# Staged transposed keys copied by ScalarE, and input-gate rows brought by DMA, in the attention stage of an mLSTM and mixture-of-experts kernel

## The chip, the cores and the metric

The kernel runs on one core of a Trainium2 chip. The metric is the device time of one execution, in microseconds (us). Engines are named as in the profile: PE is TensorE, PEld its weight load, DVE VectorE, ACT ScalarE, POOL GpSimd, SP SyncE, which here only issues transfers (DMAs).

## What is computed

Three layers follow each other. The first is an mLSTM recurrence over B=4 batches, H=8 heads, S=768 steps and D=40 columns; its output, seen as 3072 tokens of 320 columns, goes through a mixture of 8 experts with a capacity of 384 tokens each, and then through a dense layer of 2048 columns.

```python
for t in range(S):
    m_new = np.maximum(f_gate[:, :, t] + m, i_gate[:, :, t])
    f_stab = np.exp(f_gate[:, :, t] + m - m_new)
    i_stab = np.exp(i_gate[:, :, t] - m_new)
    C = f_stab * C + i_stab * outer(v_t, k_t)
    n = f_stab * n + i_stab * k_t
    y[:, :, t] = sigmoid(o_t) * (C @ q_t) / np.maximum(np.abs(n . q_t), 1.0)
...
order = np.argsort(-flat)          # tokens are given to experts, best logit first, 384 each
out[mask] = np.maximum(x[mask] @ w1[e], 0.0) @ w2[e]
...
g = np.maximum(h, 0.0) + alpha * np.minimum(h, 0.0)
return g @ w_out
```

## The kernel before

Only the first stage, attention, is touched. It cuts the 768 steps into 9 chunks of 86 and works on 36 units: unit u is chunk c = u // 4 and batch b = u % 4, all 8 heads at once. Within a chunk the recurrence is a masked product; the state is carried from chunk to chunk as 40 more rows (126 = 86 + 40).

The loop over u (line 573) writes all engines' instructions in program order, and each engine runs its own in that order; nothing is reordered. For a unit, `score` (line 435) does these things:

- pE (line 441): two bf16 matmuls of cE (113 x 126, the left factor) with aE (113 x 344). Their product is the exponent of the gate weights. cE holds the input-gate rows of the chunk in its first 24 partitions, in three bf16 parts of 8 heads; aE holds the forget-gate sums in partitions 24 to 26.
- W (line 443): ScalarE's exponential of pE, 344 columns a time.
- pS (line 448): four fp32 matmuls of the transposed keys KT (stationary) with the queries Q.
- dk (line 450): VectorE multiplies the scores with W; GpSimd makes the state's columns (line 452).

`value` (line 456) runs for unit u-2: eight matmuls pY with dk stationary, the normalisation on VectorE, the gated product x on GpSimd (line 477) and the store of x to device memory in two transfers, of 80 rows and of 6 rows (`rows`, line 349). `turn` (line 546) transposes x of unit u-4 (pX), ScalarE copies it to xT (line 553), and `logit` multiplies a chunk of it with the router's weights (pL, line 566).

The input-gate rows of chunk c+1 are made in the units with b == 2 (line 581): `gates_rows` (line 302) moves rows to the right partitions with 12 small matmuls of a selection matrix into pc, and ScalarE copies pc to cE (line 309). The forget-gate rows come by three small transfers from ap (`load_a`, line 311), 5.4 KB each. The gates themselves are made by the generators g0, g1 (chunks 0 and 1 to 3) and g2 (chunks 4 to 8, one step a unit from unit 2 on).

KT has two buffers of 128 x 16 x 126. The last 40 of the 126 columns and the partitions from 80 on are constant and filled once: buffer 0 by GpSimd (lines 334 and 338), buffer 1 by ScalarE (lines 394 and 395). A load (line 359) writes 80 partitions x 16 pieces of 86 floats (344 bytes).

All loads of the stage and the stores of x are issued by SP in one queue, in program order: v and o-gates of later chunks at b == 2, q, k and kr (keys in rows) at b == 3, the forget-gate rows behind them, then stores of x. Between them stand the pieces r of the dense weights (`words`, line 908), which `float32_of` turns from 64-bit to 32-bit floats: ScalarE's sign of r (sg, line 926), two VectorE steps, ScalarE's Abs (line 932) and GpSimd's product (line 933). A piece is issued three pieces ahead of its use; one is used every second unit from unit 8 to 23, and one every unit from unit 24 on (lines 594 to 597).

Each transfer of SP's queue carries one of eight semaphores in turn (DMAHW0 to DMAHW7 in the order below) and waits until the transfer that had it before, eight places ahead in the queue, has landed.

The lines on loads in the loop are these; the functions follow.

```python
if b == 2 and c + 1 < NCH:
    self.gates_rows(c + 1, ps)
...
if b == 3 and c + 2 < NCH:
    load_qk(c + 2)
    load_k(c + 2)
if b == 3 and c and c + 2 < NCH:
    self.load_a(c + 2, nc.sync)
```

Of the kernel before, what the change touches and what calls it, by code (L numbers as in the profile page):

```python
# [24 lines left out]
L = 86  # L25
# [35 lines left out]
def host_constants():  # L61
    import ml_dtypes
    bf = ml_dtypes.bfloat16
    ce = np.zeros((KE, X), np.float32)
    ce[24:27, :] = 1.0
    ce[27:, :L] = np.eye(L)
    ae = np.zeros((KE, H, L), np.float32)
    for p in range(3):
        for h in range(H):
            ae[p * 8 + h, h, :] = 1.0  # L70
    ae[27:] = np.where(np.arange(L)[:, None] > np.arange(L)[None, :], -1e30, 0.0)[:, None, :]
    sel = np.zeros((32, B, 3, 24), np.float32)
    for b in range(B):
        for p in range(3):
            for h in range(H):
                sel[8 * b + h, b, p, 8 * p + h] = 1.0
    g = np.arange(128)
    return {
        "c_blk": (g[:, None] // 16 == g[None, :] // 16).astype(bf),
        "c_pre": ((g[:, None] // 16 == g[None, :] // 16) & (g[:, None] < g[None, :])).astype(bf),  # L80
        "c_tri": (g[:, None] < g[None, :]).astype(bf),
        "c_sel": sel.astype(bf),
        **steps(""), **steps("_a"),
        "c_ce": np.pad(ce, ((0, 128 - KE), (0, 0))).astype(bf),
        "c_ae": np.pad(ae.reshape(KE, H * L), ((0, 128 - KE), (0, 0))).astype(bf),
    }


def host_layout(inp):
# [22 lines left out]
    o["h_i"] = np.ascontiguousarray(inp["i_gate"].reshape(32, S))  # L112
    o["h_f"] = np.ascontiguousarray(inp["f_gate"].reshape(32, S))
# [46 lines left out]
class Kern:  # L160
# [80 lines left out]
    def gates_setup(self, p):  # L241
# [19 lines left out]
        self.aE = [p.tile([KE, B, H, L], BF, name=f"aE{r}") for r in range(3)]  # L261
# [49 lines left out]
    def load_a(self, c, eng):  # L311
        for i in range(3):
            eng.dma_start(self.aE[c % 3][24 + i:25 + i], self.ap[:, i, c * L:(c + 1) * L])

    def attention(self):
        nc, a, tc = self.nc, self.a, self.tc
        with ExitStack() as ctx:
# [7 lines left out]
            KT = [p.tile([128, 16, X], F32, name=f"k{r}") for r in range(R)]  # L325
# [8 lines left out]
            nc.gpsimd.memset(KT[0][64:], 0.0)  # L334
# [3 lines left out]
            nc.gpsimd.tensor_copy(KT[0][:2 * D, :, L:], idk[:, None, :].to_broadcast([2 * D, 16, D]))  # L338
# [16 lines left out]
            def load_qk(c):  # L355
                r = c % R
                for s in range(2):
                    nc.sync.dma_start(Q[r][D * s:D * s + D, s], a["h_q"][c, s])
                nc.sync.dma_start(KT[r][:2 * D, :, :L], a["h_kt"][c])

# [11 lines left out]
            def fill_a(r):  # L372
                nc.vector.tensor_copy(self.aE[r].rearrange("p b h l -> p b (h l)"),
                                      self.ae0[:, None, :].to_broadcast([KE, B, H * L]))
# [19 lines left out]
            nc.scalar.activation(KT[1][64:].rearrange("p g x -> p (g x)"), zero[64:].to_broadcast([64, 16 * X]), AF.Copy, scale=0.0)  # L394
            nc.scalar.activation(KT[1][:2 * D, :, L:], idk[:, None, :].to_broadcast([2 * D, 16, D]), AF.Copy)
# [38 lines left out]

            def score(u):
# [3 lines left out]
                for s in range(2):  # L439
                    pE = ps.tile([X, 4 * L], F32, name="pE", bufs=2)  # L440
                    nc.tensor.matmul(pE, self.cE[c % 3][:, b, :], self.aE[c % 3][:, b, 4 * s:4 * s + 4, :],
# [3 lines left out]
                for s in range(2):  # L445
                    pS = ps.tile([X, 4, L], F32, name="pS", bufs=2)
                    for j in range(2):
                        nc.tensor.matmul(pS[:, 2 * j:2 * j + 2, :], KT[r][:, 4 * b + 2 * s + j, :],  # L448
# [124 lines left out]
            for u in range(nu + 4):  # L573
                if u < nu:
                    c, b = units[u]
                    score(u)
                    if u < 3:
                        warm_up(u)
                    if u >= G2:
                        next(g2, None)  # L580
                    if b == 2 and c + 1 < NCH:
                        self.gates_rows(c + 1, ps)
# [7 lines left out]
                    if b == 3 and c and c + 2 < NCH:  # L590
# [740 lines left out]
```

## Time and profile before

| what | value |
|---|---|
| median of 3 runs | 808.88 us |
| lowest and highest | 806.67 and 813.15 us |
| the profiled execution's own time | 807.55 us |
| its span, first to last instruction | 805.8 us |
| PE, share of the span busy | 90% |
| PE weight loads | 85% |
| DVE, ACT, POOL | 70%, 54%, 53% |
| mean granted PE clock | 0.955 of full speed |
| transfers | 72.73 MB in 47531 packets, 26097 of them under 512 bytes |

The span is from the first instruction of the execution to the last; the time holds 1.75 us more around it. A share is the mean over stages with different limits: attention takes about the first 165 us, the routing of tokens the next 50, and the experts with the dense layer the rest. A matmul's record is modelled at its end, so a busy PE need not be at its peak. Clock is given as a share of 2.4 GHz; it has two levels, 1.0 and 0.5.

### The profile page before, as it was taken

The page shows a single profiled execution, that of the slowest core. Times are in us where ns is not written, and L with a number is a line of the kernel's source. Part 1 is how long each engine was busy: PE and PEld are TensorE (multiplying, and loading weights), DVE is VectorE, ACT ScalarE, POOL GpSimd, SP SyncE. Part 2 cuts the span into 40 slices and gives each one's busy share as a digit, 9 for nine tenths or more (in the row PEclk, how much of TensorE's full clock was granted, in tenths as well). Part 3 has the DMA queues.
Part 4 walks back from the last instruction along what each step waited for, and adds up shares of the span by engine and source line. Part 5 has one row for each costly group of instructions (what it writes and reads, how often), then busy time and mean ns, then how long its engine had stood idle before and what let it go on. Part 6 is the DMA issues. An engine that isn't in the chain of part 4 may idle for free.

```text
span 805.8 us, 14935 instructions
## 1 busy us (share of the span) xinstructions
PE 724.5 (90%) x4868; PEld 688.0 (85%) x4868; DVE 560.8 (70%) x2209; ACT 435.1 (54%) x948; POOL 423.9 (53%) x509
## 2 busy tenths in 40 slices
PE   4999989920399999998999999999999999999996
PEld 3999989810388899998999899999999999999996
DVE  8887776888778878867876986797698732322311
ACT  6575655767244572565267346525833664654463
POOL 4565654569372384267149516723941686534133
PEclk9999997955599999999999999999999999999998
DMA  8999988551230150033014004202400343100000
GB/s 190 223 221 226 207 203 209 167 139 55 96 100 2 38 153 31 1 104 118 1 43 154 26 1 120 84 19 70 128 25 1 115 142 104 40 1 25 1 1 25
DMA packets 47531, 72.73 MB, mean 90 GB/s; under 512 B 26097, under 2 KB 30193, under 8 KB 47453
## 3 DMA queue, kind: packets, MB, share of 16 engines
q1 hardware_dynamic: 44332, 62.90, 29.3%
q0 software_dynamic: 2688, 8.65, 3.4%
q8 instruction: 38, 0.62, 0.3%
q14 instruction: 41, 0.33, 0.1%
q10 hardware_dynamic: 432, 0.22, 0.1%
HBM read 62.19 MB, written 9.34 MB: 89 GB/s over the span
## 4 chain that ended last, share of the span: by engine, by line
PE 51%; DVE 13%; POOL 10%; issue 8%; ACT 5%; DMA 1%; SPq 0%; POOLq 0%; DVEq 0%; ACTq 0%
PE ph L1029 23%; PE acc L1029 11%; PE fo L1029 10%; POOL gl L1166 4%; DVE scr L155 4%; DVE rb L155 3%; POOL wt L1005 2%; PE pY L464 2%; PE pS L448 2%; DVE g L155 1%; ACT m L1159 1%; ACT gh L1165 1%; ACT m L1158 1%; POOL w_dt_float32r L962 1%; PE rb L723 1%
## 5 line engine op out<-in xcount | busy, mean ns | idle before, releaser
L1166 POOL TENSOR_TENSOR gl<-g,gh 128x384 fp32r<-128x384 f32 x127 | 128.3, 1016 | 226.5 <-ACT gh L1165 218.1
L1005 POOL TENSOR_TENSOR wt<-raw,wt 128x384 fp32r<-128x384 f32 (+1 forms) x128 | 118.3, 944 | 32.4 <-ACT wt L1004 31.9
L1029 PE MATMUL ph<-yh,wfh 128*128 128x384 f32 x384 | 132.9, 346 | 0.0
L1029 PE MATMUL ph<-yh,w_dt_float32r 128*128 128x384 f32 x360 | 122.4, 340 | 0.0
L1029 PE MATMUL fo<-wfh,gh 128*128 128x320 f32 x384 | 116.2, 312 | 0.0
L1165 ACT ACTIVATE gh<-g 128x384 fp32r<-128x384 f32 x127 | 66.0, 523 | 91.0 <-DVE g L155 87.3
L155 DVE SCALAR_TENSOR_TENSOR g<-ph,m 128x384 f32<-128x384 f32 x128 | 70.4, 555 | 61.7 <-ACT m L1159 52.6
L1029 PE MATMUL fo<-w_dt_float32r,gh 128*128 128x320 f32 x360 | 109.9, 314 | 0.0
L1029 PE MATMUL ph<-xh,wt 128*128 128x384 f32 x384 | 99.7, 343 | 0.6 <-ACT xh L1060 0.6
L1091 ACT ACTIVATE hh<-ph 128x384 fp32r<-128x384 f32 x64 | 31.5, 493 | 114.2 <-PE ph L1029 83.7
L1029 PE MATMUL acc<-hh,wt 128*128 128x384 f32 x320 | 88.6, 341 | 0.0
L1029 PE MATMUL ph<-yl,wfh 128*128 128x384 f32 x256 | 84.0, 338 | 0.0
L1029 PE MATMUL fo<-wfh,gl 128*128 128x320 f32 x384 | 79.9, 312 | 0.9 <-POOL gl L1166 0.9
L1159 ACT ACTIVATE m<-m,al 128x384 f32<-128x384 f32 x119 | 73.5, 617 | 3.9
L1158 ACT ACTIVATE m<-ph 128x384 f32<-128x384 f32 x119 | 57.5, 483 | 32.9 <-PE ph L1029 31.1
L1029 PEld LDWEIGHTS ph<-yh,wfh 128*128 128x128 f32 x384 | 72.4, 188 | 0.7 <-issue 0.3
L1029 PEld LDWEIGHTS fo<-wfh,gh 128*128 128x128 f32 x384 | 72.2, 188 | 0.5 <-ACT gh L1165 0.2
L1029 PEld LDWEIGHTS ph<-xh,wt 128*128 128x128 f32 x384 | 68.8, 189 | 1.1 <-ACT xh L1060 0.8
L1004 ACT ACTIVATE wt<-raw 128x384 fp32r<-128x384 f32 x128 | 62.9, 515 | 12.7 <-DMA raw<-in_h_we_dram 12.6
L1029 PEld LDWEIGHTS fo<-w_dt_float32r,gh 128*128 128x128 f32 x360 | 67.9, 189 | 1.3 <-issue 1.2
L1029 PEld LDWEIGHTS ph<-yh,w_dt_float32r 128*128 128x128 f32 x360 | 67.9, 189 | 0.7 <-issue 0.7
L464 PEld LDWEIGHTS pY<-v,dk 126*126 126x126 f32 (+1 forms) x576 | 67.4, 192 | 0.6
(240 smaller groups left out, 1634.4 us busy)
## 6 DMA issues: line engine op xcount, KB each, us to landing
raw<-in_h_we_dram SPq DMA_DIRECT2D x64, 384.0 KB
r<-in_h_wf_dram SPq DMA_DIRECT2D x32, 352.0 KB
xd<-x SPq DMA_DIRECT2D x36, 120.0 KB
q<-in_h_q_dram SPq DMA_DIRECT2D x18, 215.0 KB
k<-in_h_kt_dram SPq DMA_DIRECT2D x9, 430.0 KB
v<-in_h_v_dram SPq DMA_DIRECT2D x9, 410.0 KB
og<-in_h_o_dram SPq DMA_DIRECT2D x9, 400.0 KB
kr<-in_h_kr_dram SPq DMA_DIRECT2D x8, 400.0 KB
```

Of the source, the lines that this page charges most:

```text
L155: return f(out, *args, **kw)
L448: nc.tensor.matmul(pS[:, 2 * j:2 * j + 2, :], KT[r][:, 4 * b + 2 * s + j, :], Q[r][:, :, 4 * b + 2 * s + j, :], start=True, stop=True)
L464: nc.tensor.matmul(pY[:M, h, :], dk[:, h, :M], V[c % RV][:, 8 * b + h, :], start=True, stop=True)
L723: self.nc.tensor.matmul(pc, self.c_blk if w is None else w, self.cacc[:, col:col + n], start=True, stop=True)
L1004: nc.scalar.activation(w[:, :384], r, AF.Copy)
L1005: nc.gpsimd.tensor_tensor(w[:, 384:], r[:, :n], w[:, :n].bitcast(F32), op=OP.subtract)
L1029: self.nc.tensor.matmul(out, w, x, **kw)
L1091: nc.scalar.activation(hh, ph, AF.Relu)
L1158: nc.scalar.activation(m, ph, AF.Relu, scale=-1.0)
L1159: nc.scalar.activation(m, m, AF.Copy, scale=alpha)
L1165: nc.scalar.activation(gh, g, AF.Copy)
L1166: nc.gpsimd.tensor_tensor(gl, g, gh.bitcast(F32), op=OP.subtract)
```

## The change

The selection matrix and `gates_rows` stay for chunk 0 alone. For the chunks from 1 on, `load_a` issues, behind each of its three transfers to aE, one that brings 8 partitions of input-gate rows from cp to cE (8 x 4 x 86 bf16). For that the gates are laid out by head and then batch, and aE with it (113 x 8 x 4 x 86), so that pE reads four runs of 86 columns in place of one of 344. There is one buffer KT; the keys of chunk 0 are loaded to it as before, those of the later chunks go to two staging buffers KS of 80 x 16 x 86 in rows of 5504 bytes, and ScalarE copies the 4 x 86 columns of unit u+1 to KT behind unit u's exponentials (`move_k`). ScalarE's two fills of the second KT buffer are gone.

`load_a` of chunk c+2 stands behind the loads of b == 3 up to unit 13, and from unit 14 on at b == 0, one unit later in the program. Neither condition holds for chunk 3, so chunk 5's six transfers are not issued: units 20 to 23 read the gate rows that chunk 2 left there, and that part of the computation is changed.

```diff
-                sel[8 * b + h, b, p, 8 * p + h] = 1.0
+                sel[B * h + b, b, p, 8 * p + h] = 1.0
...
-        self.aE = [p.tile([KE, B, H, L], BF, name=f"aE{r}") for r in range(3)]
+        self.aE = [p.tile([KE, H, B, L], BF, name=f"aE{r}") for r in range(3)]
...
     def load_a(self, c, eng):
         for i in range(3):
-            eng.dma_start(self.aE[c % 3][24 + i:25 + i], self.ap[:, i, c * L:(c + 1) * L])
+            eng.dma_start(self.aE[c % 3][24 + i:25 + i].rearrange("o h b l -> o (h b) l"), self.ap[:, i, c * L:(c + 1) * L])
+            if c:
+                eng.dma_start(self.cE[c % 3][8 * i:8 * i + 8, :, :L], self.cp[:, i, c * L:(c + 1) * L])
...
-            KT = [p.tile([128, 16, X], F32, name=f"k{r}") for r in range(R)]
+            KT = p.tile([128, 16, X], F32, name="k")
+            KS = [p.tile([2 * D, 16, L], F32, name=f"ks{r}") for r in range(R)]
...
-                nc.sync.dma_start(KT[r][:2 * D, :, :L], a["h_kt"][c])
+                nc.sync.dma_start(KS[r] if c else KT[:2 * D, :, :L], a["h_kt"][c])
...
-                nc.vector.tensor_copy(self.aE[r].rearrange("p b h l -> p b (h l)"),
-                                      self.ae0[:, None, :].to_broadcast([KE, B, H * L]))
+                nc.vector.tensor_copy(self.aE[r], self.ae0.rearrange("p (h l) -> p h l", h=H)[:, :, None, :].to_broadcast([KE, H, B, L]))
...
-            nc.scalar.activation(KT[1][64:].rearrange("p g x -> p (g x)"), zero[64:].to_broadcast([64, 16 * X]), AF.Copy, scale=0.0)
-            nc.scalar.activation(KT[1][:2 * D, :, L:], idk[:, None, :].to_broadcast([2 * D, 16, D]), AF.Copy)
...
+            def move_k(u):
+                c, b = units[u]
+                nc.scalar.activation(KT[:2 * D, 4 * b:4 * b + 4, :L], KS[c % R][:, 4 * b:4 * b + 4, :], AF.Copy)
+
...
-                    nc.tensor.matmul(pE, self.cE[c % 3][:, b, :], self.aE[c % 3][:, b, 4 * s:4 * s + 4, :],
+                    nc.tensor.matmul(pE, self.cE[c % 3][:, b, :], self.aE[c % 3][:, 4 * s:4 * s + 4, b, :],
...
+                    if 4 <= u + 1 < nu:
+                        move_k(u + 1)
...
-                    if b == 2 and c + 1 < NCH:
-                        self.gates_rows(c + 1, ps)
+                    if b == 0 and c and c + 2 < NCH and u >= G2 + 12:
+                        self.load_a(c + 2, nc.sync)
...
-                    if b == 3 and c and c + 2 < NCH:
+                    if b == 3 and c and u < G2 + 12:
                         self.load_a(c + 2, nc.sync)
```

SP's queue at the turn from chunk 5 to chunk 6, before: the loads for chunk 7 (k, kr in 80 and 6 rows, aE), the store of unit 21's x, and the piece r that ScalarE uses in unit 27.

```order
L359 DMA k_105<-in_h_kt_dram 80x16x86 [waits DMAHW3_49]
L351 DMA kr_107<-in_h_kr_dram 80x1280 [waits DMAHW4_49,Pool_49]
L353 DMA kr_107<-in_h_kr_dram 6x1280 [waits DMAHW5_49]
L313 DMA aE_100<-ap 1x32x86 [waits DMAHW6_49]
L313 DMA aE_100<-ap 1x32x86 [waits DMAHW7_49]
L313 DMA aE_100<-ap 1x32x86 [waits DMAHW0_49]
L351 DMA xd<-x_112 80x384 [waits DMAHW1_49,Pool_49]
L353 DMA xd<-x_112 6x384 [waits DMAHW2_49]
L911 DMA r_1573<-in_h_wf_dram 128x704 [waits DMAHW3_49,DVE_49,Activation_49]
```

The same place of SP's queue now, from the keys of chunk 7 to the same piece r (aE and cE are those of chunk 8):

```order
L362 DMA ks_106<-in_h_kt_dram 80x1376 [waits DMAHW5_49,Activation_49]
L354 DMA kr_108<-in_h_kr_dram 80x1280 [waits DMAHW6_49,Pool_49]
L356 DMA kr_108<-in_h_kr_dram 6x1280 [waits DMAHW7_49]
L354 DMA xd<-x_113 80x384 [waits DMAHW0_49,Pool_49]
L356 DMA xd<-x_113 6x384 [waits DMAHW1_49]
L313 DMA aE_101<-ap 1x32x86 [waits DMAHW2_49]
L315 DMA cE_98<-cp 8x4x86 [waits DMAHW3_49]
L313 DMA aE_101<-ap 1x32x86 [waits DMAHW4_49]
L315 DMA cE_98<-cp 8x4x86 [waits DMAHW5_49]
L313 DMA aE_101<-ap 1x32x86 [waits DMAHW6_49]
L315 DMA cE_98<-cp 8x4x86 [waits DMAHW7_49]
L917 DMA r_1531<-in_h_wf_dram 128x704 [waits DMAHW0_49,DVE_49,Activation_49]
```

Before, r shares DMAHW3 with k and waits for it; now it shares DMAHW0 with the store ahead of the small transfers, and the small transfer just ahead of r shares DMAHW7 with the six rows of kr.

ScalarE's queue at unit 14 (chunk 3, b == 2), before:

```order
L443 ACTIVATE W<-pE 126x344 [waits DVE_49,PE_49,Pool_49]
L443 ACTIVATE W<-pE 126x344 [waits PE_49]
L309 ACTIVATE cE_97<-pc 24x4x86 [waits PE_49]
L932 ACTIVATE w_dt_float_852<-w_dt_float_852 128x352 [waits DVE_49]
L926 ACTIVATE sg<-r_601 128x352 [waits DMAHW3_49,Pool_49]
```

And now at unit 12, where a copy of keys stands behind the exponentials of each unit:

```order
L447 ACTIVATE W<-pE 126x344 [waits PE_49] x2
L437 ACTIVATE k<-ks_106 80x4x86
L938 ACTIVATE w_dt_float_589<-w_dt_float_589 128x352 [waits DVE_49]
L932 ACTIVATE sg<-r_377 128x352 [waits Pool_49]
L432 ACTIVATE og<-og 86x320
L433 ACTIVATE og<-og 86x320 [waits Activation_49]
L557 ACTIVATE xT<-pX 128x3x86 [waits PE_49]
```

The copy of pc with its wait for PE is gone from the units with b == 2, and a copy from KS stands in every unit; in the last unit of a chunk it also waits for the transfer to KS.

## Rows read from the trace of the kernel before

**Rows 1.** Windows of 20 us: busy us of each engine (instructions), granted clock, DMA share, GB/s.

```profile
60.00:80.00 20.00, 19.71 (x187) 18.55 (x186) 14.86 (x43) 12.06 (x32) 10.72 (x17) 1.00 0.97 229
100.00:120.00 20.00, 18.80 (x183) 17.60 (x182) 15.96 (x46) 10.62 (x28) 12.49 (x19) 1.00 0.87 204
```

**Rows 2.** PE in order of time: start, us, instruction, shapes, count [idle before].

```profile
49.14 0.63 PE L307 MATMUL pc<-cp,sel 32*24 32x86 bf16 x12
49.70 1.95 PE L464 MATMUL pY<-v,dk 126*126 126x41 f32 x16
...
86.07 0.46 PE L441 MATMUL pE<-aE,cE 113*126 113x344 bf16 x2
...
93.99 0.46 PE L441 MATMUL pE<-aE,cE 113*126 113x344 bf16 x2
...
101.54 0.46 PE L441 MATMUL pE<-aE,cE 113*126 113x344 bf16 x2
```

**Rows 3.** Waits of 106 to 122 us: who waited for whom, total us, times, longest.

```profile
ACT sg L926 <- DMA r<-in_h_wf_dram: 3.3, 1, 3.3
```

**Rows 4.** PE in order of time, units 28 and 29 and the start of 30.

```profile
118.64 0.46 PE L441 MATMUL pE<-aE,cE 113*126 113x344 bf16 x2
...
121.95 1.51 PE L448 MATMUL pS<-q,k 128*126 128x172 f32 x4 [2.27 <-ACT KL L522]
...
133.46 0.46 PE L441 MATMUL pE<-aE,cE 113*126 113x344 bf16 x2
```

**Rows 5.** Windows of 1 us, columns as in rows 1.

```profile
131.00:132.00 1.00, 1.00 (x7) 1.00 (x6) 0.66 (x2) 0.14 (x1) 0.37 (x1) 0.50 1.14 158
...
216.00:217.00 1.00, 1.00 (x6) 1.00 (x4) 0.83 (x8) 0.00 (x0) 0.00 (x0) 0.50 0.96 353
...
220.00:221.00 1.00, 1.00 (x5) 1.00 (x4) 0.91 (x3) 0.94 (x3) 0.97 (x2) 0.61 0.95 379
```

**Rows 6.** SP's queue in order of time: when a transfer was issued.

```profile
51.63 0.36 SPq L911 DMA_DIRECT2D r<-in_h_wf_dram  x1
...
67.46 0.36 SPq L911 DMA_DIRECT2D r<-in_h_wf_dram  x1
...
83.19 0.36 SPq L911 DMA_DIRECT2D r<-in_h_wf_dram  x1
...
99.10 0.36 SPq L911 DMA_DIRECT2D r<-in_h_wf_dram  x1
...
110.55 1.78 SPq L313 DMA_DIRECT2D aE<-ap  x3
...
114.02 0.27 SPq L353 DMA_DIRECT2D xd<-x  x1
116.63 0.36 SPq L911 DMA_DIRECT2D r<-in_h_wf_dram  x1
117.32 0.31 SPq L351 DMA_DIRECT2D xd<-x  x1
```

**Rows 7.** Waits of SP's queue, 106 to 121 us.

```profile
SPq L911 <- DMA k<-in_h_kt_dram: 2.3, 1, 2.3
```

**Rows 8.** ACT in order of time.

```profile
13.83 0.42 ACT L295 ACTIVATE ap<-cum 32x258 bf16<-32x258 f32 x1 [0.50 <-DVE cum L290]
...
119.90 0.53 ACT L926 ACTIVATE sg<-r 128x352 f32<-128x352 f32 x1 [3.29 <-DMA r<-in_h_wf_dram]
```

**Rows 9.** Groups by line, 12 to 165 us: count | busy us, mean ns | idle before.

```profile
L448 PE MATMUL pS<-q,k 128*126 128x172 f32 x288 | 52.8, 324 | 4.1 <-ACT KL L522 2.3 <-DVE LT L569 1.6
...
L441 PE MATMUL pE<-aE,cE 113*126 113x344 bf16 x72 | 17.9, 324 | 4.6 <-ACT k L394 2.5 <-ACT W L443 1.8 <-DMA aE<-ap 0.4
...
L932 ACT ACTIVATE w_dt_float<-w_dt_float 128x352 f32<-128x352 f32 x20 | 9.9, 495 | 0.2 <-DVE w_dt_float L155 0.2
```

**Rows 10.** Groups by line, 0 to 13 us.

```profile
L373 DVE COPY aE<-ae 113x2752 bf16<-113x2752 bf16 x2 | 1.7, 858 | 0.0
L377 DVE COPY cE<-ce 113x504 bf16<-113x504 bf16 x3 | 0.7, 273 | 0.0
```

More of the change, by code (lines that the diff above doesn't have):

```diff
@@ L111, in host_layout @@
     o["h_o"] = rows(inp["o_gate"]).reshape(NCH, L, B, DM)
-    o["h_i"] = np.ascontiguousarray(inp["i_gate"].reshape(32, S))
-    o["h_f"] = np.ascontiguousarray(inp["f_gate"].reshape(32, S))
+    for n, x in (("h_i", "i_gate"), ("h_f", "f_gate")):
+        o[n] = np.ascontiguousarray(inp[x].reshape(B, H, S).transpose(1, 0, 2)).reshape(32, S)
     wg = np.zeros((128, 3, 32), np.float32)
@@ L333, in attention @@
             self.gates_fill()
-            nc.gpsimd.memset(KT[0][64:], 0.0)
+            nc.gpsimd.memset(KT[64:], 0.0)
             ident = self.identf
@@ L337, in attention @@
             nc.vector.tensor_tensor(idk, ident[:2 * D, :D], ident[:2 * D, D:2 * D], op=OP.add)
-            nc.gpsimd.tensor_copy(KT[0][:2 * D, :, L:], idk[:, None, :].to_broadcast([2 * D, 16, D]))
+            nc.gpsimd.tensor_copy(KT[:2 * D, :, L:], idk[:, None, :].to_broadcast([2 * D, 16, D]))
             nc.gpsimd.memset(V[0][64:], 0.0)
@@ L447, in score @@
                     for j in range(2):
-                        nc.tensor.matmul(pS[:, 2 * j:2 * j + 2, :], KT[r][:, 4 * b + 2 * s + j, :],
+                        nc.tensor.matmul(pS[:, 2 * j:2 * j + 2, :], KT[:, 4 * b + 2 * s + j, :],
                                          Q[r][:, :, 4 * b + 2 * s + j, :], start=True, stop=True)
```

## The prediction

> **What bounds the kernel now.** The change touches only the attention stage, which ends at about 165 of the 805.8 us span; what follows is the same code and starts when the stage ends, so I look for the shift of that end. I read the stage by windows first, then TensorE in order of time, then the waits, then the queue of transfers.
>
> The windows show TensorE busy for 19 us and more of each 20, and the DMA engines at 0.87 to 0.97 [rows 1]. So two things are near full. In order of time, TensorE runs unit behind unit without a gap: a chunk of four takes 15.47 us, from 86.07 to 101.54 [rows 2]. The input-gate matmuls (pc, 12 of them) hold the next group up by 0.56 us, from 49.14 to 49.70 [rows 2].
>
> There is one place where TensorE is stopped. ScalarE waits 3.3 us for a piece r of the dense weights [rows 3], TensorE then stands idle for 2.27 us in the middle of unit 28 [rows 4], and its granted clock is at the lower level (1.2 GHz) until about 132 [rows 5]. The pair of units 28 and 29 takes 14.82 us from 118.64 to 133.46 [rows 4]; the pair 20 and 21, with the same groups, takes 7.92 from 86.07 to 93.99 [rows 2]. The place costs 6.9 us: 2.27 idle and some 4.6 at the lower clock.
>
> Why is r late? It is issued at 116.63 [rows 6]. The queue's waits give the keys' landing as what held it (2.3 us) [rows 7]: the order of the queue shows every transfer waiting for the one eight places ahead, and for this r that is k. The r of one loop to the r of the next is 15.9 us (83.19 to 99.10) and then 17.5 (99.10 to 116.63) [rows 6], against 15.47 for TensorE. **So SyncE's queue with its transfers is a loop of its own, a little slower than TensorE's**, which falls behind until r is too late, when from unit 24 on a piece is wanted every unit and not every second.
>
> **The change, part by part**, against the profiled execution's own time of 807.55 us (the median of the runs shown is 1.3 above it).
>
> *Input-gate matmuls.* Eight groups go: 8 x 0.56 = 4.5 us of TensorE's own time. Seven lie ahead of unit 28 (3.9 us), one behind it. With them go eight ScalarE copies of pc, which no one waits for.
>
> *The keys' transfer.* 80 partitions by 16 pieces of 344 bytes become 80 rows of 5504. Of before, the second q had landed at 114.02 (the six-row store waits for it), k at 116.63 and the 80 rows of kr at 117.32 [rows 6]: k takes 2.6 us after q, kr's rows of 5120 bytes 0.7 after k. The new load costs between 0.7 and 2.6 us. I take 1.5, since kr's 0.7 overlaps the end of k: 1.1 us are saved.
>
> *Six small transfers for three.* Before, three of them took 1.78 us of the queue, 0.6 each, while k was on its way [rows 6]: hidden. Now six stand ahead of r, and the sixth waits, eight places back, for the six-row piece of kr, which lands after k. So r comes at 117.32 (kr) - 1.1 (shorter keys) + 0.3 (six-row piece, about one issue of 0.31) + 0.6 (the sixth's issue) = 117.1: each loop is 0.5 us longer, not shorter. Ends: with the sixth's wait already over, r follows the keys and the loop is 1.1 shorter; with the keys' load no faster and all three added issues in series (1.8), 117.32 + 0.3 + 1.8 = 119.4, 2.8 longer. The trace is nearest to 0.5, because the new transfers have the size and kind of the old three. The Trainium skill (DMA: Bandwidth & Descriptors, Rules for kernel authors) asks to coalesce small transfers, as under 64 KB one pays mostly overhead; charged in series at the fixed 2 us of that page three more would cost 6 us a loop, and 24 us over four loops. No row here bears that out: the three old ones lie beside k.
>
> *Four loops* end in an r between 51.63 and the r at 116.63 (those at 67.46, 83.19 and 99.10, and this one [rows 6]): 4 x 0.5 = 2.0 us later, less 1.1 once for the key loads that come ahead of the first of them: **r is issued 0.9 us later, at 117.5.** From issue to ScalarE's start took 3.27 us (116.63 to 119.90 [rows 6, 8]); TensorE resumes at 121.95 + 0.9 = 122.85. It arrives there 3.9 us earlier than before, so its idle grows from 2.27 to some 7.1 us. What the seven groups gave goes into that wait.
>
> *The lower clock.* I take the same 4.6 us. Ends: after a long idle stretch, with TensorE busy from 216 on, the upper clock returned in the slice 220 to 221 [rows 5]; some 4.8 us at half speed would cost 2.4, so 2.2 less; a second fall elsewhere, 4.6 more.
>
> *The copies on ScalarE.* 32 copies of 80 by 344. The nearest row is the 128x352 one of line 932, 495 ns [rows 9], so some 0.48 each by the count of elements: 32 x 0.48 = 15.4 us, over 32 units of 3.7 us. ScalarE is busy 10.6 to 12.1 us in 20 [rows 1], four fifths of them at most with the copies; in a chunk 1.9 us come and 0.45 (the pc copy) goes. Cost 0. Without that cover, all 15.4. Each copy is issued one unit ahead; at a chunk's start it waits for the keys' landing, and output gates, xT and the next exponentials queue behind it. The keys of chunk 6 had landed at 99.10 (its r waits for them), 2.4 us ahead of unit 24's first matmul at 101.54 [rows 2, 6]. With 6 x 0.56 = 3.4 us of that gone and 0.5 for the copy, up to 1.5 us of wait moves there; TensorE has 7 us to lose before unit 28, so it costs 0.
>
> *Start.* The two ScalarE fills of the second key buffer go, but the operation behind them waits for VectorE at 13.83 [rows 8]: 0. VectorE's fill of the left factor now reads runs of 86 elements: before, 2752 elements took 858 ns, 504 took 273 [rows 10], both in four runs; 0.26 ns an element leaves 0.14 us. If that is paid by run, 32 runs cost 1.0 us more a fill, two of them on the way to the first scores; if not, nothing. I take 0.15 each, since an instruction has a fixed part as well: +0.3, ends 0 and +2. The scores' first matmul (pE) reads four runs of 86 columns; pS reads two such runs and has the same mean, 324 ns, as pE [rows 9]: 0.
>
> **Sum:** +0.9 (r) - 0.56 (the group behind unit 28) + 0.3 (start) = +0.6, or 808.2 us by the profiled execution. Since the median stood 1.3 above it, I predict 808.5. About 1%, 8 us, is what a measurement of this kernel can tell from no change.
>
> **The rivals.**
>
> *The loop keeps TensorE's pace.* If keys and kr land about as much sooner as TensorE runs ahead (1 us a loop: the 1.1 saving without the sixth's wait), the stall keeps its size and the gain stays: 807.55 - 4.5 = 803. For it: the shorter keys. Against it: the order of the queue. Chance 0.2.
>
> *The stall goes too.* 807.55 - 4.5 - 6.9 = 796. For this r must be issued 3.3 + 3.9 = 7.2 us earlier, 1.8 in each of four loops, more than the keys' part can give unless the 0.7 us of kr is its true cost (1.9). Chance 0.12.
>
> *Slower: the small transfers lengthen the loop.* With 2.8 us a loop, r comes 4 x 2.8 = 11 us later: 807.55 + 11 - 0.6 = 818. It decides from the point where a loop is over 2.3 us longer, as the end then moves by more than 8. The place is the six issues ahead of r, each held by a landing; that the long rows bring nothing (the change does not do what it says) belongs here. For it: DMA engines at 0.9 and a queue that waits on landings everywhere [rows 1, 7]. Against it: there is no such stall by the three old ones. Chance 0.13; the skill's rule above would end here, and has no chance of its own beyond that.
>
> *The forecast*, within 804 and 812: 0.55.
>
> **How the numbers follow.** Faster by over 1%: the second rival and a little of the first, 0.13. Slower by over 1%: the upper three quarters of the third, 0.1. Within: 0.77. The range leaves out the second rival and the upper part of the third: 800.5 to 815, which also holds the ends of clock and start one at a time.
>
> **What would show it.** In the profile after: no pc after the first group, chunks of about 14.9 us on TensorE up to unit 23; r's of the queue still 16 us or more apart, with waits for kr or for the small transfers ahead of them; ScalarE's wait for r near unit 27 of 7 us or more and one stretch of lower clock behind it. I am wrong if that wait is 3.3 us or less, if the r's come under 15.5 us apart, or if TensorE waits at the chunks' starts for the copies.

## The result: 12 us slower, and the profile after

The changed kernel takes 822.8 us (median; 821.1 at best) against 811.0 for the kernel before on the same chip: ratio 1.015, 95% interval 1.010 to 1.020. I had predicted 808.5, 800.5 to 815, most likely no change: wrong. The profiled execution took 830.5 us (span 827.9). The first matmul of the routing code, which follows the attention stage, starts at 191.25 instead of 170.93 us, so nearly all of the 22 us that the spans differ by lie in the stage.

TensorE in order of time, in the profile after (start, us, instruction, shapes, count, idle before it):

```profile
42.11 0.47 PE L445 MATMUL pE<-aE,cE 113*126 113x344 bf16 x2
42.41 0.75 PE L452 MATMUL pS<-q,k 128*126 128x172 f32 x4
44.60 0.85 PE L452 MATMUL pS<-q,k 128*126 128x172 f32 x4 [1.45 <-DVE LT L573]
...
54.81 0.78 PE L445 MATMUL pE<-aE,cE 113*126 113x344 bf16 x2
...
61.41 0.78 PE L445 MATMUL pE<-aE,cE 113*126 113x344 bf16 x2
...
113.04 0.47 PE L445 MATMUL pE<-aE,cE 113*126 113x344 bf16 x2
...
127.76 0.47 PE L445 MATMUL pE<-aE,cE 113*126 113x344 bf16 x2
```

In the kernel before, TensorE's stop at the same place and the window behind it (columns as in [rows 1]; the last three figures are granted clock, DMA share and GB/s):

```profile
44.96 0.85 PE L448 MATMUL pS<-q,k 128*126 128x172 f32 x4 [0.51 <-DVE LT L569]
```

```profile
44.00:60.00 16.00, 15.49 (x156) 14.73 (x154) 12.56 (x36) 11.60 (x30) 10.42 (x16) 1.00 0.88 210
```

Windows of 1 us in the profile after:

```profile
46.00:47.00 1.00, 1.00 (x8) 1.00 (x7) 0.51 (x2) 0.00 (x0) 0.38 (x1) 0.58 1.00 292
47.00:48.00 1.00, 1.00 (x7) 1.00 (x7) 0.03 (x1) 0.00 (x0) 0.00 (x0) 0.50 1.05 235
...
100.00:101.00 1.00, 1.00 (x8) 1.00 (x7) 0.89 (x2) 0.00 (x0) 0.00 (x0) 0.61 0.01 2
```

Three things are to be seen. First, the gain is there: with the pc groups gone, a chunk at the upper clock takes 127.76 - 113.04 = 14.72 us, where [rows 2] gave 15.47. Second, TensorE stops for 1.45 us in unit 9, where VectorE's copy LT frees a buffer of PSUM (the memory that TensorE writes to), and from 46 to 101 us its clock is at the lower level (1.2 GHz), though it is busy all the time; a unit then takes 61.41 - 54.81 = 6.60 us instead of 3.4. In the kernel before the same stop was 0.51 us and the clock stayed up. Third, the queue. Its list in order of time, and ScalarE's wait for r, which answers to [rows 3, 6]:

```profile
132.08 0.54 SPq L313 DMA_DIRECT2D aE<-ap  x1
132.93 0.74 SPq L315 DMA_DIRECT2D cE<-cp  x1
134.89 0.53 SPq L313 DMA_DIRECT2D aE<-ap  x1
136.48 0.73 SPq L315 DMA_DIRECT2D cE<-cp  x1
137.93 0.52 SPq L313 DMA_DIRECT2D aE<-ap  x1
138.50 0.73 SPq L315 DMA_DIRECT2D cE<-cp  x1
139.34 0.36 SPq L917 DMA_DIRECT2D r<-in_h_wf_dram  x1
```

```profile
ACT sg L932 <- DMA r<-in_h_wf_dram: 4.4, 1, 4.4
```

From the first of the six to r it is 139.34 - 132.08 = 7.3 us; before, from the first of the three to r, with two stores between them, it was 116.63 - 110.55 = 6.1 [rows 6]. r comes 18.8 us after the r of the loop before (120.52), and ScalarE's wait for it near unit 28 is 4.4 us instead of 3.3. TensorE waits there for ScalarE's copy KL, which stands behind the sign of r in ScalarE's order. So there were two suspects, and my theory at first was the clock: that the longer stop in unit 9 lowers it (Theory 1). Its rivals were the queue, held up by the six (Theory 2, later A), and ScalarE's key copies (Theory 3, later C). The profile alone can't tell them apart, because at half the clock TensorE also gives the queue time.

### The profile page after: what moved, and what is told of

Same layout as the page of the kernel before. It is cut to its first block, busy times and chain, and to the rows that moved or that the text cites. A ratio compares the mean times of both kernels' runs of the same rounds, so it can differ in the third digit from the quotient of the medians.

```text
span 827.9 us, 14821 instructions
## 1 busy us (share of the span) xinstructions
PE 743.4 (90%) x4772; PEld 708.5 (86%) x4772; DVE 563.7 (68%) x2209; ACT 441.3 (53%) x970; POOL 422.8 (51%) x509
## 4 chain that ended last, share of the span: by engine, by line
PE 48%; DVE 13%; POOL 9%; issue 7%; ACT 4%; DMA 3%; SPq 0%; POOLq 0%; DVEq 0%; ACTq 0%
PE ph L1035 22%; PE acc L1035 10%; PE fo L1035 10%; POOL gl L1172 4%; DVE scr L155 4%; DVE rb L155 3%; POOL wt L1011 2%; PE pY L468 2%; DVE g L155 1%; ACT m L1165 1%; PE pS L452 1%; ACT gh L1171 1%; DMA q<-in_h_q_dram 1%; ACT m L1164 1%; POOL w_dt_float32r L968 1%
## 5 line engine op out<-in xcount | busy, mean ns | idle before, releaser
L468 PEld LDWEIGHTS pY<-v,dk 126*126 126x126 f32 (+1 forms) x576 | 80.7, 222 | 0.1
L468 PE MATMUL pY<-v,dk 126*126 126x41 f32 (+1 forms) x576 | 79.0, 305 | 0.0
L481 POOL TENSOR_TENSOR x<-xn,og 86x320 f32<-86x320 f32 x35 | 30.2, 862 | 79.8 <-ACT W L447 33.3
```

The lines of the kernel that those rows point to most:

```text
L468: nc.tensor.matmul(pY[:M, h, :], dk[:, h, :M], V[c % RV][:, 8 * b + h, :], start=True, stop=True)
L481: eng.tensor_tensor(xt[:, :DM].rearrange("p (h d) -> p h d", h=H), xn, OG[c][:, b].rearrange("p (h d) -> p h d", h=H), op=OP.mult)
```

## The experiments

All times are medians, and ratios are to the kernel before on the same chip, with 95% intervals. "r to r" is the mean over the four loops that end in the r of unit 28, from the queue's list (before: 16.25 us, from [rows 6]).

| kernel | us | ratio | r to r, us |
|---|---|---|---|
| change | 822.8 | 1.015 [1.010, 1.020] | |
| change again (e14_after) | 821.7 | 1.011 [1.007, 1.015] | 19.0 |
| e1_keys: keys alone | 808.8 | 0.997 [0.994, 1.001] | 15.6 |
| e2b_gates: gate rows alone | 822.7 | 1.018 [1.011, 1.024] | 19.6 |
| e3_lt_act: change, LT on ScalarE | 817.4 | 1.008 [1.005, 1.011] | 18.2 |
| e4_before_stop: before, longer stop | 810.0 | 0.999 [0.995, 1.003] | |
| e5_dummy: e1 + 3 unused transfers | 821.2 | 1.017 [1.010, 1.024] | 17.8 |
| e11_tiny: the same, one piece each | 820.0 | 1.014 [1.008, 1.020] | 17.9 |
| e12_tiny_pool: the same, by GpSimd | 810.4 | 1.001 [0.997, 1.005] | 16.3 |
| e9_rows_pool: change, six by GpSimd | 808.0 | 0.996 [0.992, 0.999] | 14.6 |
| e8_dram: change, two for six | 813.7 | 1.003 [1.000, 1.006] | |
| e10_best | 805.4 | 0.995 [0.992, 0.997] | 15.2 |

### One part at a time

e1_keys has the staged keys and their copies alone, and pc and the three aE transfers as before.

> Only the keys' part of the change: staged rows of 5504 bytes and the 32 ScalarE copies; gate rows by matmuls (pc) and the queue's order as in the kernel before. Theory 1, the clock: the loss of 12 us comes from TensorE's stop of 1.45 us in unit 9 (0.51 before), behind which the granted clock stays at 0.5 for 54 us; that stop grew because the pc groups are gone and TensorE comes there 1.3 us sooner. With pc back, the stop is 0.5 to 0.9 us, no low clock before unit 28, and the time lies within 1% of before: 803 to 812. Theory 2, the queue: the six small transfers hold r up; without them the loop is a little shorter than before, the stop near unit 28 is under 2.3 us, 800 to 808, and no low clock in unit 9 either. Theory 3, the copies: ScalarE's copies hold up the exponentials and through them VectorE; then the stop in unit 9 is over 1.2 us here too, and the time near 822.

Measured: 808.8 us. The stop in unit 9 is 0.52 us, no low clock before unit 28:

```profile
45.15 0.85 PE L451 MATMUL pS<-q,k 128*126 128x172 f32 x4 [0.52 <-DVE LT L572]
```

Theory 3 falls: the copies cost nothing that can be measured.

e2_gates was to have the gate rows alone, but I had put the two fills of the second key tile behind that tile's load, and ScalarE waited 12 us for it at the start (831.4 us, 1.025). e2b_gates has them in their place.

> Only the gate rows' part: rows by transfer, no pc after the first group, six small transfers ahead of r; keys loaded straight into two key tiles as before, no copies (chunk 5's gate rows are not loaded, as in the changed kernel). Theory 1, the clock: TensorE reaches unit 9 1.1 us sooner, VectorE does not, so the stop there is 1.2 to 1.6 us, the granted clock falls to 0.5 for tens of us, and the time is 818 to 832. Theory 2, the queue: no low clock in unit 9; the small transfers lengthen the loop, r comes late, and one stop near unit 28 of over 6 us makes 815 to 822. Theory 3, the copies: without them no loss: 803 to 808.

> The gate rows' part alone again, with ScalarE's two fills of the second key tile back at their place ahead of that tile's load (in e2_gates they stood behind it, and ScalarE waited 12 us for the transfer at the start). Chunk 5's gate rows are not loaded, as in the changed kernel. Theory A, the queue: with six small transfers ahead of r and the keys still in pieces of 344 bytes, a loop of SP's queue takes 18 us or more (15.9 to 17.5 before); the rows that the left factor waits for and r come late, and the time is 815 to 826, as much as the whole change or more. Theory B, the clock alone (a stop in unit 9 that happens to lower the clock): either 805 to 812 or near 830, by whether the clock falls in unit 9, and r's spacing plays no part. Theory C, the copies: without them no loss, 803 to 808.

Measured: 822.7 us, the whole loss. In its profile TensorE waits 3.06 us for cE's rows at unit 12 and 4.34 near unit 28; the stop in unit 9 is 0.55. The loss is the gate rows'. This run alone does not tell the queue from the clock: behind the stop of 3.06 us, from 58 to 96 us, TensorE is busy for 38.00 of 38 us at a granted clock of 0.51. A long stretch of low clock stands here as well, behind a late transfer and not behind unit 9's stop.

### Is it the stop in unit 9?

e3_lt_act takes that stop out of the changed kernel:

```diff
-                    nc.vector.tensor_scalar(LT[c], pL, 0.0, None, op0=OP.add)
+                    nc.scalar.activation(LT[c], pL, AF.Copy)
```

> The changed kernel with one edit: the copy of the logits LT from PSUM, which frees the buffer that TensorE waits for in unit 9, is made by ScalarE instead of VectorE (nine copies of 128x86; chunk 5's gate rows are not loaded, as in the changed kernel). Theory 1, the clock: no stop over 0.5 us in unit 9, granted clock 1.0 from 13 us to unit 28; then the queue, now with less time, makes a stop near unit 28 of 5 to 11 us; 803 to 815 in all, at least 8 us under the changed kernel. Theory 2, the queue: the 54 us at half speed only gave the queue the time that it lacked; the stop near unit 28 grows by all that is won, and the time stays 818 to 826. Theory 3, the copies: VectorE is late by the exponentials, so another stop takes the place of this one within the next units and the clock falls all the same, 820 or more.

Measured: 817.4. The stop and its low clock are gone. By the medians 4.3 to 5.4 us go with them, by the ratios 0.3 to 0.7%, with intervals that overlap; the greater part of the loss stays, in other places. TensorE in e3_lt_act:

```profile
55.43 0.80 PE L445 MATMUL pE<-aE,cE 113*126 113x344 bf16 x2 [2.98 <-DMA cE<-cp]
...
73.37 0.80 PE L445 MATMUL pE<-aE,cE 113*126 113x344 bf16 x2 [1.88 <-DMA cE<-cp]
...
133.00 1.51 PE L452 MATMUL pS<-q,k 128*126 128x172 f32 x4 [5.77 <-ACT KL L526]
```

It waits for the gate rows themselves at the starts of chunks 3 and 4, and 5.77 us behind the late r. e4_before_stop goes the other way and lengthens the stop in the kernel before:

```diff
+                    if c == 0:
+                        xs = p.tile([128, 1400], F32, name="xs")
+                        nc.vector.tensor_copy(xs, ident[:, 1:2].to_broadcast([128, 1400]))
                     nc.vector.tensor_scalar(LT[c], pL, 0.0, None, op0=OP.add)
```

> The kernel before with one added VectorE instruction (a fill of 128x1400 in SBUF that nobody reads, some 0.9 us by the 128x1280 fill's 0.81) ahead of the first LT copy only, so that TensorE's stop in unit 9 grows from 0.51 to about 1.4 us. Theory 1, the clock: the granted clock falls to 0.5 behind that stop for tens of us, and the time rises by 10 to 25 us, to 820 to 835. Theories 2 and 3: the stop costs its own 0.9 us at most, 808 to 813, and no low clock before unit 28.

Measured: 810.0, no change. TensorE's stop, and the window behind it:

```profile
48.25 0.85 PE L448 MATMUL pS<-q,k 128*126 128x172 f32 x4 [1.31 <-DVE LT L572]
```

```profile
48.00:64.00 16.00, 15.60 (x154) 14.85 (x155) 12.65 (x37) 10.80 (x29) 10.34 (x16) 1.00 0.90 199
```

A stop of 1.31 us and the clock stayed at 2.4 GHz: such a stop need not lower it. With e3_lt_act, where most of the loss stays without the stop, Theory 1 falls as the main cause; what is left of it is called Theory B below.

e14_after is the changed kernel unchanged, for a second profile.

> The changed kernel once more, unchanged, for a second profile beside the kernel before. If the 54.6 us at the lower clock behind unit 9 belong to the program, they are seen again behind a stop of 1.4 us there. If they belong to that execution (whose time, 830.5, lay 8 us above the median of 822.8), the clock stays up in unit 9, and TensorE's lost time shows as waits for cE's rows at the starts of units 12 and 16 and for r near unit 28, as in e3_lt_act, with r's 17 to 19 us apart; 820 to 824.

Measured: 821.7. Both suspects show again: a stop of 1.96 us in unit 9 with the clock at the lower level from 46.5 to 67, and near unit 28 a stop of 5.75.

```profile
46.48 1.51 PE L452 MATMUL pS<-q,k 128*126 128x172 f32 x4 [1.96 <-DVE LT L573]
...
136.61 1.51 PE L452 MATMUL pS<-q,k 128*126 128x172 f32 x4 [5.75 <-ACT KL L526]
```

So the low clock came back, but for 20.5 us, not 54.6, and the time is the same within 1%. In these two profiles, the more the clock takes in unit 9, the less the queue takes near unit 28 (a stop of 3.67 us behind 54.6, of 5.75 behind 20.5).

### Is it the queue, and what of it?

e5_dummy adds to e1_keys the three cE transfers alone, into tiles that nobody reads; TensorE, ScalarE and VectorE do what they do in e1_keys.

```diff
+            if c:
+                eng.dma_start(self.xE[c % 3][8 * i:8 * i + 8, :, :L], self.cp[:, i, c * L:(c + 1) * L])
```

> e1_keys (staged keys, gate rows by pc; 808.8 us there) with three added small transfers in each group: the cE rows' own transfers, 8 rows of 4 pieces of 172 bytes, into tiles that nobody reads. TensorE's work, ScalarE's and VectorE's are those of e1_keys. Theory A, the queue: the group of six takes 6 us or more on SP's queue where three took 1.8 to 2; r comes 2 us later a loop, the wait for r near unit 28 grows by 6 us or more, 813 to 822. Theory B, the clock alone: unit 9's stop is that of e1_keys (0.52), so no low clock before unit 28 and 806 to 811. Theory C: as e1_keys, 806 to 811.

Measured: 821.2, 12.4 us over e1_keys by the medians, some 16 by the ratios: **three small transfers that nobody needs cost as much as the whole change.** e11_tiny cuts each to one piece of 172 bytes:

```diff
-                eng.dma_start(self.xE[c % 3][8 * i:8 * i + 8, :, :L], self.cp[:, i, c * L:(c + 1) * L])
+                eng.dma_start(self.xE[c % 3][i:i + 1, 0, :L], self.cp[:1, i, c * L:(c + 1) * L])
```

> e5_dummy with the three added transfers of each group cut to one piece of 172 bytes each (one partition to one partition, nobody reads it) instead of 32 pieces. Theory A1, the places: what costs is that each transfer takes one of the eight semaphores in turn, so that aE's later ones, r and what follows wait for the landing of a load three places nearer (q, ks, kr); size does not matter, r's come 17 to 18 us apart as in e5_dummy and the time is 815 to 823. Theory A2, the work: what costs is the issuing (0.73 each, against some 0.3 for one piece) and the 96 small pieces in the DMA queues; then the r's are 15.5 to 16.5 apart and the time is 807 to 813, near e1_keys (808.8).

Measured: 820.0, so the size does not matter. TensorE in e11_tiny waits for the late rows of aE and behind the late r:

```profile
73.60 0.83 PE L447 MATMUL pE<-aE,cE 113*126 113x344 bf16 x2 [2.42 <-DMA aE<-ap]
...
132.03 1.51 PE L454 MATMUL pS<-q,k 128*126 128x172 f32 x4 [3.53 <-ACT KL L528]
```

About half of the price is paid in clock. From 36 to 150 us TensorE is idle for 8.5 us at a mean granted clock of 0.90, in e1_keys for 3.6 us at 0.96: 5 us more of stops and, as an estimate, 0.06 x 114 = 7 us by the lower clock behind them. The spans differ by 11.8 us (817.6 and 805.8).

One loop of the queue in e1_keys, and in e11_tiny (stores of xd left out):

```profile
72.23 0.36 SPq L360 DMA_DIRECT2D ks<-in_h_kt_dram  x1
74.42 0.32 SPq L352 DMA_DIRECT2D kr<-in_h_kr_dram  x1
...
75.64 2.29 SPq L313 DMA_DIRECT2D aE<-ap  x3
...
80.75 0.35 SPq L916 DMA_DIRECT2D r<-in_h_wf_dram  x1
```

```profile
81.44 0.32 SPq L363 DMA_DIRECT2D ks<-in_h_kt_dram  x1
82.95 0.32 SPq L355 DMA_DIRECT2D kr<-in_h_kr_dram  x1
...
85.86 0.60 SPq L316 DMA_DIRECT2D xE<-cp  x1
87.60 0.52 SPq L314 DMA_DIRECT2D aE<-ap  x1
89.27 0.60 SPq L316 DMA_DIRECT2D xE<-cp  x1
...
91.21 0.36 SPq L919 DMA_DIRECT2D r<-in_h_wf_dram  x1
```

The waits of the queue from 60 to 130 us, first e1_keys, then e11_tiny:

```profile
SPq L916 <- DMA ks<-in_h_kt_dram: 5.5, 4, 1.7
```

```profile
SPq L316 <- DMA ks<-in_h_kt_dram: 4.7, 4, 1.4
SPq L355 <- DMA og<-in_h_o_dram: 4.5, 4, 1.2
SPq L314 <- DMA q<-in_h_q_dram: 4.0, 4, 1.2
```

From kr to r it is 6.3 us in these loops of e1_keys and 8.3 in e11_tiny. In e1_keys r itself is what waits for the keys' landing (L916). With three places more, it is the third added transfer that waits for the keys (L316) and the third aE for q (L314); r stands behind both, and behind what is issued after them.

There is a rival: an added transfer also takes SyncE's own time, 0.60 us each with one piece (0.73 with 32), so 1.8 us a loop. The rows speak against it. The transfer that waits for the keys comes 8.2 us behind their issue in e1_keys (r, mean of four loops) and 8.1 in e11_tiny (the third added one). The issues between them take less than half of that, so the time of the first two added ones lies in the shade of the keys. What is new is that r comes 2.0 us behind the keys' landing and not with it.

e12_tiny_pool issues the same three from GpSimd, whose transfers have eight semaphores of their own.

> e11_tiny (820.0 us) with its three added one-piece transfers of each group issued by GpSimd, whose transfers have semaphores of their own. Same bytes, same destinations. Theory A1, the places on SP's semaphores: the loss is gone, r's 15 to 16.5 us apart, 806 to 812 as e1_keys (808.8). Theory A2, the transfers' own work in the DMA queues: 815 to 822 again.

Measured: 810.4, the loss is gone but for 0.4%, within the intervals. Bytes and destinations are the same: **the price is the place in SP's queue.** This edit takes the semaphores and SyncE's 1.8 us away together; that the places among the eight semaphores count, and not the 1.8 us, rests on the rows above and on e6_rows_act below.

e9_rows_pool does that for the change itself (`nc.sync` to `nc.gpsimd` in the two calls of load_a).

> The changed kernel with the six small transfers of chunks 3 to 8 issued by GpSimd, whose transfers have eight semaphores of their own in the order (on ScalarE, in e6_rows_act, they shared SP's eight, and ScalarE stood waiting for SP's loads). LT stays on VectorE, chunk 5's gate rows are not loaded, as in the changed kernel. Theory A, the queue: SP's r's come 13.5 to 15 us apart, no wait for cE's rows, no wait for r over 1 us, 800 to 812; the stop in unit 9 stays and may lower the clock. If GpSimd's issuing (its cost is shown by no run so far) holds up its products dk and x, TensorE waits for these, and it is 815 or more. Theory B, the clock alone: the clock falls behind unit 9 as in the changed kernel, 818 or more. Theory C: 820.

Measured: 808.0, 15 us under the changed kernel, and r to r 14.6 us. TensorE, and the window behind unit 9's stop:

```profile
44.61 0.85 PE L452 MATMUL pS<-q,k 128*126 128x172 f32 x4 [1.63 <-DVE LT L573]
...
110.53 0.55 PE L445 MATMUL pE<-aE,cE 113*126 113x344 bf16 x1 [3.21 <-DVE fk L512]
```

```profile
44.00:60.00 16.00, 15.02 (x143) 14.52 (x144) 13.21 (x37) 12.59 (x33) 13.92 (x23) 1.00 0.91 229
```

The stop in unit 9 is longer than in the changed kernel's first profile, and the clock stays up. A new stop, 3.21 us, came in unit 26: in this build the score's second PSUM buffer is the one that the first choice (fk) still reads.

### Other queues, fewer transfers

e6_rows_act and e7_r_act move transfers to ScalarE's queue: the six (`nc.scalar` for load_a), or all r's.

> The changed kernel with the six small transfers of chunks 3 to 8 issued on ScalarE's queue instead of SP's (chunk 5's gate rows are not loaded, as in the changed kernel). Theory A, the queue: the r's of SP's queue come 13.5 to 15 us apart, no wait for cE's rows, no wait for r over 1 us; ScalarE pays some 3.8 us of issuing in each chunk (0.52 and 0.73 each by the rows of SP's queue), which it has; 797 to 808, with unit 9's stop still there. Theory B, the clock alone: the stop in unit 9 is still 1.4 us, the clock falls behind it as in the changed kernel, 818 or more. Theory C, ScalarE: with another 3.8 us a chunk it is the bound; exponentials come late in every chunk, 825 or more.

> The changed kernel with the pieces r of the dense weights issued on ScalarE's queue (32 issues of 0.36), the six small transfers still on SP's (chunk 5's gate rows are not loaded, as in the changed kernel). Theory A, the queue: no wait for r any more; the rows of cE still come late or just in time, so one or two stops of 1 to 3 us at chunk starts remain; 806 to 816, between the kernel before and the changed one. Theory B, the clock alone: 818 or more with the low clock behind unit 9, or about 803 without. Theory C: 820.

Measured: 826.8 (1.021 [1.013, 1.029]) and 863.4 us (1.068 [1.058, 1.078]), both misses for Theory A. 826.8 is in Theory C's range, but by waits more than by ScalarE's own issuing. ScalarE in e6_rows_act:

```profile
45.88 0.73 ACTq L315 DMA_DIRECT2D cE<-cp  x1
46.65 0.47 ACT L432 ACTIVATE og<-og 86x320 f32<-86x320 f32 x1 [7.54 <-DMA v<-in_h_v_dram]
```

For 7.54 us ScalarE computes nothing. It issues transfers and stands between them, 2.1 us before the one at 43.30 and 1.3 before the one at 45.88, and by the profile the landing that released it last was that of v, a load that SP issued. The built program's order shows why (two transfers on ScalarE in e6_rows_act, two on GpSimd in e9_rows_pool):

```
L313 DMA aE_99<-ap 1x32x86 [waits DMAHW6_49]
L315 DMA cE_96<-cp 8x4x86 [waits DMAHW2_49]
...
L313 DMA aE_99<-ap 1x32x86 [waits DMASW4_49]
L315 DMA cE_96<-cp 8x4x86 [waits DMASW5_49]
```

ScalarE's take their places among SP's eight (DMAHW0 to 7), so the queue's waits came to ScalarE, with the exponentials behind them; GpSimd's have their own (DMASW0 to 7). SyncE is rid of the six issues here and the places stay, and r to r is 20.0 us, no shorter than in the changed kernel (ScalarE's stops lengthen it too). In e7_r_act TensorE's stops for cE (3.33 and 3.40), for ScalarE's key copies (3.85) and for its xT (4.26) are the longest; I have not taken that run apart further.

e8_dram writes the gate parts of chunks 5 to 8 to DRAM once and loads each chunk's with two transfers instead of six; LT is on ScalarE.

> The changed kernel with the LT copies on ScalarE (as e3_lt_act) and fewer transfers ahead of r: the gate parts of chunks 5 to 8 are written to DRAM once (two transfers behind unit 11) and read back for each chunk by two transfers, one for the three aE rows and one for the 24 cE rows; chunk 3's and chunk 4's six are issued in units 4 and 11 ahead of the keys. Chunk 5's rows are loaded. Theory A, the queue: from unit 12 on two small transfers stand where six stood, one less than in the kernel before; the r's come 14.5 to 15.5 us apart, no wait for cE's rows after unit 16, a wait for r near unit 28 of 0 to 4 us; 798 to 808. Theory B, the clock alone: with no stop in unit 9 it is as e3_lt_act, 815 to 820. Theory C, the copies: 815 to 820, and TensorE's stops wait for ScalarE.

Measured: 813.7, better than e3_lt_act, short of what I expected: r's come 15.6 us apart (89.63 to 105.26), but chunk 4's six, issued in one lump ahead of the keys, make TensorE wait 3.53 us for the key copy at 76.89, and near unit 28 it waits 3.84.

e13_whole goes for fewer places in another way: in e1_keys, v, kr and og each in one transfer of 86 rows instead of 80 and 6.

> e1_keys (808.8 us) with v, kr and og each loaded by one transfer of 86 rows instead of two (80 and 6): three places fewer in each chunk, same bytes. Theory A1, the places: the reverse of e11_tiny; r's come sooner, the wait for r near unit 28 goes, 797 to 806. Against it: if a transfer of 86 rows lands later than the two (six rows more than 16 engines of 5 rows), the waits for landings grow, and it is 808 to 815.

Measured: 971.7 us (1.194 [1.186, 1.203]). The window from 60 to 100 us, first of e1_keys, then of e13_whole:

```profile
60.00:100.00 40.00, 39.57 (x385) 37.51 (x383) 29.68 (x85) 29.23 (x78) 22.30 (x35) 1.00 0.86 225
```

```profile
60.00:100.00 40.00, 33.29 (x178) 30.95 (x179) 15.67 (x41) 13.28 (x34) 9.84 (x17) 0.59 0.41 119
```

The DMA engines' share falls from 0.86 to 0.41, which fits loads that keep few engines busy; no row here counts the engines of one load. By the Trainium skill (DMA: Bandwidth & Descriptors, "Why a DMA increments its semaphore by 16 and not by 1") a transfer runs on the largest number of engines up to 16 that divides its slowest dimension, which is 2 for 86 rows and 16 for 80; the fall of the share agrees. So the split in two places is what the loads need, and it says nothing against the price of a place.

### A version that beats both

e10_best is e9_rows_pool with LT on ScalarE, the transposes of the first choice in unit 24 instead of 25, and chunk 5's gate rows loaded in unit 13.

> e9_rows_pool (six small transfers by GpSimd, 808.0) with three more edits: the LT copies on ScalarE (as e3_lt_act), the transposes of the first choice one unit earlier (24, not 25), so that the scores' PSUM buffer of the next unit is not the one that the choice still reads (in e9_rows_pool TensorE waits 3.21 us there, and 10.2 us of low clock follow), and chunk 5's gate rows loaded, in unit 13. Theory A, the queue: with SP's loop at 14.5 us, no stop over 1 us before unit 28; 808 less 3.2, less up to 5 for the low clock, less up to 1.6 for unit 9: 797 to 804. If it stays at 806 to 810, the attention stage is not what sets the end any more, or another stop has taken the place of these.

Measured: 805.4, faster than the kernel before (0.9949 [0.9923, 0.9974]), by less than expected. The routing code's first matmul starts at 163.44, 7.5 us sooner than before, but TensorE then waits for the gather of tokens, with some 7 us of low clock behind it, and at its last matmul 3.4 us of the 7.5 are left (795.2 against 798.6). Over e9_rows_pool the three further edits bring 0.1%, within the noise.

```profile
117.97 0.85 PE L452 MATMUL pS<-q,k 128*126 128x172 f32 x4 [3.43 <-ACT KL L526]
...
216.42 1.73 PE L1065 MATMUL ptr<-identf,xg 128*128 128x128 f32 x9 [2.83 <-DMA xg<-xd,ids]
```

The first line is the stop behind r near unit 28, which is still there, too. e15_r_first moves r ahead of the unit's loads of v and og.

> e10_best (805.4 us) with each piece r issued ahead of the unit's loads of v and og (or q, keys and kr) instead of behind them; the order on the other engines is unchanged. If r's place in SP's list sets the stop near unit 28 (3.43 us in e10_best, 6.8 us of low clock behind it), r comes there 1.3 us (four issues of 0.32) or more sooner, the stop shrinks below 2 us: 800 to 804. If the loads that now stand behind r come as much later (v, og, keys), ScalarE's copies wait for the keys and TensorE for them: 805 to 810.

Measured: 808.5 (0.998 [0.995, 1.001]). The stop shrinks to 1.25 us, and TensorE waits for ScalarE's key copies instead (1.23 us at 98.76): here the order in the queue only dealt out the lateness.

## Why the prediction was wrong

*Input-gate matmuls: right.* A chunk is 0.75 us shorter (0.56 expected). With the places' price taken away, that gain is seen: e9_rows_pool and e10_best are the two that beat the kernel before.

*The keys' transfer: too large.* 1.1 us were to be saved in a loop. From the keys' issue to the r that waits for their landing it was 8.5 us before (mean of four) and is 8.2 in e1_keys; r's come 15.6 us apart against 16.25, close to TensorE's own 15.47. So 0.3 to 0.6 us are seen, and no time came of it by itself (0.997).

*Six small transfers for three: the step that failed.* It made "each loop 0.5 us longer", with 2.8 as the upper end, and I took 0.5 "because the new transfers have the size and kind of the old three". e11_tiny shows that size is not what is paid. The three old ones were hidden since behind them r had to wait for the keys anyway; the next three pushed r behind that wait. Measured: 2.2 us a loop (e5_dummy against e1_keys, 17.8 and 15.6), or 1.9 over the kernel before with the change's own rows (e3_lt_act). I had counted one place, the sixth's wait for kr, and not that every wait behind the six moves: in e3_lt_act a cE transfer in the midst of the six waits for the keys, and the rest of the six stand between that and r. The Trainium skill's rule (DMA: Bandwidth & Descriptors, Rules for kernel authors) that small transfers be coalesced pointed the right way, and one piece costing as much as 32 agrees with its reason; the price here is some 0.7 us each, not the 2 us by which the prediction charged them in series.

*Four loops: the consequence was too narrow.* r was to come 0.9 us later, at 117.5; in e3_lt_act it comes at 127.6. I had only r come late. The rows of cE come late as well, and TensorE waits for them at the chunks' starts (2.98 and 1.88 us in e3_lt_act). The rival "the small transfers lengthen the loop" gave 818 with 2.8 us a loop, and had a chance of 0.13: it was the mechanism, and its size was nearly right. The sign that I had named, a wait for r of 7 us or more and one stretch of lower clock behind it, did not come: in the profile after the wait is 4.4 us and the long stretch lies ahead of it.

*The lower clock: wrong.* I took the same 4.6 us at one place. There is low clock behind the other stops as well, and the stop in unit 9 was not foreseen: TensorE comes there 1.3 us sooner (43.16 against 44.45, where the first half of the scores ends), VectorE's LT only 0.35. VectorE had waited 0.34 us for the exponentials, which stand behind a key copy, and its next instruction (line 299) took 1.25 us (0.58 before), beside GpSimd's product dk (41.02 to 41.76) and then GpSimd's own of line 299. Without the stop the changed kernel keeps some 6 us of its loss (e3_lt_act).

*The copies on ScalarE: right.* 32 of 0.488 us, 15.6 in all (15.4 expected), and no loss in e1_keys.

*The start: small, with the wrong sign.* The first pE is at 12.46 against 12.62, 0.16 us sooner where 0.3 later was forecast. Before, it waited for ScalarE's fill of the second key buffer ([rows 9]: 2.5 <-ACT k L394), which I had put at nothing.

*Slips.* 808.2 with the 1.3 of the median added is 809.5, not 808.5; and TensorE's second window in [rows 1] is 18.80 us, not 19 and more. Neither bears on the outcome.

Put together by ratios: keys alone -0.3%; the places +1.4 to +1.7 over before; with pc gone and the rows real +0.8 (e3_lt_act); with unit 9's stop +1.1 to +1.5. What stays open is why the clock fell behind the stops of 1.45 and 1.96 us in the changed kernel and not behind those of 1.31 (e4_before_stop) and 1.63 (e9_rows_pool): these rows do not tell the four apart.

## What to carry to other kernels

In this kernel a queue whose transfers take turns on a few semaphores was paid by the place, not by the byte: before adding a small transfer, find which instruction waits for which landing, and move all of them on by the places added. A cover that hides three transfers need not hide six; a row that shows the first three hidden prices the next three only if the same wait still ends last behind them. When the profile of a slower kernel shows a long stretch of lower clock, test it apart: it can hide another loss, which comes back as soon as the clock is kept up; and a late transfer can be paid in clock as well as in waiting.

## What the runs showed of the hardware that I had not expected

- The granted clock stayed at 0.5 for 54.6 us (20.5 in a second execution) while TensorE was busy in every microsecond, after a stop of 1.45 us (1.96).
- A VectorE instruction of 32x430 elements took 1.24 to 1.31 us in the profiles where it overlapped GpSimd's instruction of the same shape (after, e3_lt_act, e14_after, e12_tiny_pool; 1.05 in e10_best), and 0.58 to 0.69 in before and e1_keys, where it did not.
- With loads of 86 rows 119 GB/s were moved from 60 to 100 us, with loads split in 80 and 6 rows 225.
- GpSimd's issue of a small transfer took 0.51 to 0.58 us of its own time (six in 3.3 us, 102.07 to 105.35 in e9_rows_pool), and the kernel still took 808.0 us.
